# Dense layers on float16 halves with scales taken from the data, and every weight chunk used once for all 1792 tokens

## The chip, the cores and the metric

The kernel runs on one core of a Trainium2 chip. The metric is the device time of one execution in microseconds (us); before the change it is 1415.47 us, the median of 3 runs between 1414.61 and 1416.2. The engines are TensorE (PE in the profile, its weight loads PEld), VectorE (DVE), ScalarE (ACT), GpSimd (POOL) and SyncE (SP), which here only issues DMAs.

## The reference

Talking-heads attention, then two dense blocks on its result (1792 tokens = 4 batches x 448, width 768 = 12 heads x 64):

```python
scores = einsum('bhij,hg->bgij', q @ k.T * 0.125, w_pre)
attn = softmax(scores)
x = einsum('bhij,hg->bgij', attn, w_post) @ v     # -> [1792, 768]
h = (x @ w1) * (x @ w2)                           # w1, w2: 768 x 1024
x2 = h @ w3 @ w_out                               # 1024 x 1024, 1024 x 768
g = relu(x2 @ w_in) ** 2                          # 768 x 2048
out = g @ moe2_w_out                              # 2048 x 768, float32
```

The attention inputs are float32. The dense weights arrive as float64, and the kernel reads them as pairs of int32.

## The kernel before

The first part, up to about 493 us, is the attention: 180 blocks (16 supers of 11 or 12 blocks, four to a batch) in an order written out by hand, slot by slot, with later steps attached to slots by `at()`. Of it only its output step matters here: `put_x` (L452) scales the finished rows on ACT and sends them to DRAM as float32 (`xT_d`), `regroup` (L259) is a DMA that each block needs four slots ahead, and `load_x` (L688) brings x back for the dense part.

The dense part is scheduled by the Tile framework, engine by engine, from the order of the code. Its products take float32 in two fp32r parts, a high one (`wh`, `hh`) and the rest (`wl`, `ll`), and add three matmuls: high x high, high x low, low x high (`product`, L784, 448 columns; `layer_out`, L904, and `m_pair`, L809, 384 columns). A weight chunk is decoded from float64 by two ACT activations, an integer step, a clamp, a second integer step on DVE, an Abs on ACT and a product with the sign on DVE (L622 to L632); then ACT rounds the high part (L661) and POOL subtracts (L662).

The tokens go through in two halves of 896 (the loop `for hf in range(NH)`). Half 0 decodes each chunk and keeps the decoded float32 in DRAM (`kept_*`, L654); half 1 loads these again and splits them on ACT and DVE (L648, L649). Once, between the w1/w2 products and x2 of half 0, M = w3 @ w_out is formed from 384 matmuls and put into DRAM (`M_d`); x2 = h @ M. In the last part p runs over 8 pairs of chunks: `layer_in(2p)`, `layer_in(2p+1)` and then `layer_out(p-1)`, whose products DVE adds into the accumulator (L912; at p = 0 ACT copies, L910). PSUM gives the dense part 8 banks (`mm`).

Of the kernel before, what the change touches and what calls it, by code (L numbers as in the profile page):

```python
# [1 line left out]

# [26 lines left out]
WO_AT = (1, 2, 4, 5)  # L29


@with_exitstack
def talking_heads_attention_moe_moe2(
# [39 lines left out]
    xT_d = dram.tile([DM, NT], F32, name="xT_d")  # L73
    M_d = dram.tile([NDC, P, NFC * P], F32, name="M_d")
# [7 lines left out]
    const = ctx.enter_context(tc.tile_pool(name="const", bufs=1))  # L82
    sp = ctx.enter_context(tc.tile_pool(name="sp", bufs=2))
# [303 lines left out]
    def scale_v(b, hg, i):  # L387
        m = vsum[b, hg]
        if i == 0:
            nc.vector.tensor_reduce(m[:CP, 3:4], m[:CP, 0:3], axis=AX.X, op=ALU.max)  # L390
        elif i == 1:
            vps[b, hg] = pt = psum(ps_p, "p")
            nc.tensor.transpose(pt[:1, :CP], m[:CP, 3:4], ident[:CP, :CP])
        elif i == 2:
            pt = vps.pop((b, hg))
            nc.vector.tensor_reduce(m[:1, 4:5], pt[:1, :CP], axis=AX.X, op=ALU.max)
        elif i == 3:
            vps[b, hg] = pt = psum(ps_p, "p")
# [99 lines left out]
    for b in range(B):  # L498
        f = first[4 * b]
        for hg, o in ((0, 2), (1, 8)):  # L500
            at(f + o - 5, LOAD, load_v, b, hg)
            for i in range(3):
                at(f + o + i + 1, MID, sum_v, b, hg, i)
                at(f + o + i + 9, MID, split_v, b, hg, i)
                at(f + o + i + 10, LOW, split_vl, b, hg, i)
            for i, (slot, kind) in enumerate(((4, MID), (5, END), (6, MID), (7, END), (8, MID))):
                at(f + o + slot, kind, scale_v, b, hg, i)
    for s in range(NSUP - 1):
        L = -(-SUP[s + 1][2] // NR)
# [39 lines left out]
    for hf in range(NH):  # L549
        for fc in range(NFC):  # L550
            chunks += [("w1", hf, fc), ("w2", hf, fc)]
            if hf == 0 and fc in WO_AT:
                j = 2 * WO_AT.index(fc)
                chunks += [("wo", 0, j), ("wo", 0, j + 1)]
        if hf == 0:
            for p in range(NFC // 2):
                for g in range(2):
                    chunks += [("w3", 0, 4 * p + 2 * j + g) for j in range(2)]
                if p == 0:
                    chunks += [("wo", 1, f) for f in range(NFC // 2, NFC)]  # L560
        for c in range(NDC):
            chunks += [("m", hf, 2 * c), ("m", hf, 2 * c + 1)]
        for p in range(NP2):
            chunks += [("in", hf, 2 * p), ("in", hf, 2 * p + 1)]
            if p > 0:
                chunks += [("out", hf, 2 * p - 2), ("out", hf, 2 * p - 1)]
        chunks += [("out", hf, NF2 - 2), ("out", hf, NF2 - 1)]
# [8 lines left out]
    limit = [place["wo", 1, NFC // 2]]

    def in_place(i):
        return chunks[i][0] == "m" or chunks[i][1] > 0

    def wtile(z):
        return pools["w"].tile([P, DM], F32R, tag=f"w{z}", name=f"w{z}", bufs=WBUFS)

    def load_w(i):
        kind, hf, j = chunks[i]
        cs = slice(j * P, (j + 1) * P)
        if in_place(i):
            if kind == "wo":
                t = wo_tiles(j)[1]
            else:  # L590
                t = wtile("l")
            if kind == "m":
                c, g = divmod(j, 2)
                lo, hi = (0, MF * P) if g == 0 else (MF * P, (NFC if hf else NFC - 2) * P)
                t = t[:, : hi - lo]
                nc.sync.dma_start(t.bitcast(F32), M_d[c][:, lo:hi])
            else:
                nc.sync.dma_start(t.bitcast(F32), kept[kind, j])
            wraw[i] = t
            return  # L600
        t = pools["w"].tile([P, 2 * DM], I32, tag="raw", name="raw", bufs=LOADS)
        if kind in ("out", "wo"):
            src = {"out": moe2_w_out, "wo": moe_w_out}[kind].bitcast(I32)
            nc.sync.dma_start(t, src[cs, :])
        elif kind == "w3":
            f, g = divmod(j, 2)
            t = t[:, : 8 * P]
            nc.sync.dma_start(t, moe_w3.bitcast(I32)[f, g])
        else:
            src = {"w1": moe_w1, "w2": moe_w2, "in": moe2_w_in}[kind].bitcast(I32)  # L610
            nc.sync.dma_start(t, src[j])
        wraw[i] = t

    def decode(raw, n):
# [381 lines left out]
```

## Time and profile before

| | |
|---|---|
| median of 3 runs | 1415.47 us (1414.61 to 1416.2) |
| the profiled execution's own time | 1411.23 us |
| its span, first to last instruction | 1409.5 us |
| mean granted TensorE clock | 0.985 |
| PE busy | 1358.5 us, 96% of the span, 10176 matmuls |
| DVE / ACT / POOL busy | 983.7 (70%) / 745.2 (53%) / 497.9 us (35%) |
| HBM read / written | 100.49 MB / 34.60 MB |

A share of busy time is a mean over stages: attention, then w1/w2, M, x2 and in/out. A matmul's duration in the timeline is a latency; matmuls overlap, and what each costs is the distance between two starts. In the tables of windows the columns are busy us and number of instructions of each engine, then the granted clock (1.00 is the 2.4 GHz level, 0.50 the 1.2 GHz level), the share of time in which the DMA engines work, and GB/s.

### The profile page before, as it was taken

What the parts mean: (1) busy time and instruction counts of PE and PEld (TensorE: products, weight loads), DVE (VectorE), ACT (ScalarE), POOL (GpSimd) and SP (SyncE); (2) the same over time, 40 slices, a digit from 0 to 9 for tenths busy, and PEclk for the clock granted to TensorE, in tenths of its full rate; (3) what the DMA queues carried; (4) which work ended last, traced back from release to release, by engine and by line L of the source; (5) the groups of instructions that cost most, each with busy time, mean ns of one, the idle gap of its engine ahead of it and who ended that gap; (6) DMA issues with size and microseconds to landing.
All of it is one profiled execution on the core that took longest, in us unless ns stands there. A gap on an engine that the chain in (4) does not pass through costs nothing. (4 is left out here: it accounts for less than half of the span.)

```text
span 1409.5 us, 26306 instructions
## 1 busy us (share of the span) xinstructions
PE 1358.5 (96%) x10176; PEld 1155.9 (82%) x10176; DVE 983.7 (70%) x1688; ACT 745.2 (53%) x1363; POOL 497.9 (35%) x489
## 2 busy tenths in 40 slices
PE   5999999999998799889999999999999999999999
PEld 3566666666665599789999999999999999999998
DVE  6998999999898877865627788998322224355555
ACT  3877877877875766665526655554222223422220
POOL 3789789789775623222102222221000000000000
PEclk8999999999999799999999999999999999999999
DMA  5345445455537456644524344434211121111112
GB/s 174 109 136 151 117 136 154 127 138 145 143 89 226 147 188 204 221 160 135 189 73 169 129 174 169 157 124 162 96 57 53 38 66 57 57 45 47 66 57 90
DMA packets 82512, 175.32 MB, mean 124 GB/s; under 512 B 19412, under 2 KB 51540, under 8 KB 82388
## 3 DMA queue, kind: packets, MB, share of 16 engines
q1 hardware_dynamic: 82388, 173.65, 39.5%
q8 instruction: 80, 1.31, 0.4%
q14 instruction: 44, 0.36, 0.1%
HBM read 100.49 MB, written 34.60 MB: 96 GB/s over the span
## 5 line engine op out<-in xcount | busy, mean ns | idle before, releaser
L784 PE MATMUL mm<-hl,wh 128*128 128x448 f32 x1536 | 443.8, 370 | 2.6 <-ACT wh L661 1.5
L784 PEld LDWEIGHTS mm<-hl,wh 128*128 128x128 f32 x1536 | 290.1, 189 | 31.0 <-ACT wh L661 2.2
L784 PE MATMUL mm<-hl,wl 128*128 128x448 f32 x768 | 284.4, 370 | 2.9 <-POOL wl L662 2.9
L904 PE MATMUL mm<-wh,act 128*128 128x384 f32 x896 | 231.8, 337 | 0.9 <-ACT act L910 0.6
L339 PEld LDWEIGHTS <-EH 120*112 120x112 f16 (+1 forms) x1440 | 134.5, 132 | 86.9 <-issue 86.6
L265 PE MATMUL p<-Bt,wpre_k 120*120 120x448 f32 x360 | 183.6, 593 | 15.7 <-DMA Bt<-S 13.0
L327 POOL TENSOR_TENSOR EL<-E,EH 120x448 f16<-120x448 f32 x180 | 191.4, 1064 | 15.0
L662 POOL TENSOR_TENSOR wl<-xa,wh 128x768 fp32r<-128x768 f32 x48 | 89.9, 1880 | 288.3 <-ACT wh L661 261.6
L904 PEld LDWEIGHTS mm<-wh,act 128*128 128x128 f32 x896 | 162.2, 188 | 2.8 <-DVE act L912 1.3
L324 POOL TENSOR_SCALAR E<-E,st 120x448 f32<-120x448 f32 x180 | 135.4, 752 | 75.1 <-DVE EH L316 33.8
L784 PEld LDWEIGHTS mm<-hl,wl 128*128 128x128 f32 x768 | 145.3, 189 | 17.8 <-POOL wl L662 3.7
L904 PE MATMUL mm<-wl,act 128*128 128x384 f32 x448 | 150.6, 336 | 0.0
L287 ACT ACTIVATE E<-p,st 120x448 f32<-120x448 f32 x180 | 115.3, 640 | 58.6 <-DVE st L279 46.4
L648 ACT CAST wh<-wl 128x768 fp32r<-128x768 f32 (+1 forms) x72 | 53.5, 746 | 156.0 <-DMA wl<-kept_out 73.2
L339 PE MATMUL o<-wph,EH 120*112 120x120 f16 x720 | 127.2, 219 | 7.3 <-DVE ATl L361 6.8
L339 PE MATMUL o<-wph,EL 120*112 120x120 f16 x720 | 127.0, 219 | 3.1 <-POOL EL L327 2.8
L912 DVE TENSOR_TENSOR act<-act,mm 128x384 f32<-128x384 f32 x196 | 103.1, 550 | 37.9 <-PE mm L904 37.2
L279 DVE TENSOR_REDUCE st<-p 120x1 f32<-120x448 f32 x180 | 110.9, 616 | 25.7 <-PE p L265 23.9
L339 PE MATMUL o<-wpl,EH 120*112 120x120 f16 x720 | 127.1, 219 | 0.0
L649 DVE TENSOR_TENSOR wl<-wl,wh 128x768 fp32r<-128x768 f32 (+1 forms) x72 | 60.4, 845 | 90.7 <-ACT wh L648 88.2
L355 ACT CAST ATh<-o 112x480 f16<-112x480 f32 x180 | 100.9, 560 | 43.0 <-PE o L339 42.1
L316 DVE TENSOR_SCALAR EH<-E,st 120x448 f16<-120x448 f32 x180 | 121.2, 673 | 2.9
(128 smaller groups left out, 2490.7 us busy)
## 6 DMA issues: line engine op xcount, KB each, us to landing
Bt<-S SPq DMA_DIRECT2D x176, 210.0 KB
raw<-in_moe_w_out_dram SPq DMA_DIRECT2D x24, 768.0 KB
raw<-in_moe_w_dram SPq DMA_DIRECT2D x16, 768.0 KB
raw<-in_moe_w_in_dram SPq DMA_DIRECT2D x16, 768.0 KB
raw<-in_moe_w_dram SPq DMA_DIRECT2D x16, 512.0 KB
kept_w<-xa SPq DMA_DIRECT2D x16, 384.0 KB
kept_in<-xa SPq DMA_DIRECT2D x16, 384.0 KB
kept_out<-xa SPq DMA_DIRECT2D x16, 384.0 KB
```

The lines of the kernel that those rows point to most:

```text
L265: nc.tensor.matmul(pt[: n * H, :S], wpre_k.rearrange("p t g -> p (t g)")[: n * H, : n * H], Bt.pop(u)[: n * H], start=True, stop=True,)
L279: nc.vector.tensor_reduce(nsum[u][:n, 0, j : j + 1], Pp[u][:n, :S], axis=AX.X, op=ALU.max, negate=True)
L287: nc.scalar.activation(e[:n], Pp.pop(u)[:n, :S].rearrange("p (a b) -> p a b", a=EG), AF.Exp, bias=t[:n, 0, j : j + 1], scale=1.0, accum_ou ...
L316: nc.vector.tensor_scalar(hh[:n].rearrange("p (a b) -> p a b", a=EG), Ex[u][:n], inverse(u), None, op0=ALU.mult)
L324: nc.gpsimd.tensor_scalar(e, e, inverse(u), 1.0, op0=ALU.mult, op1=ALU.mult)
L327: nc.gpsimd.tensor_tensor(a, e, b, op=ALU.subtract)
L339: nc.tensor.matmul(pt[:CP, c * n : (c + 1) * n], a[:n, c * CP : (c + 1) * CP], w[:n, :n], start=(i == 0), stop=(i == 2),)
L355: nc.scalar.copy(ATs[s][0][:, :, :, m * NR : m * NR + nr], src)
L662: nc.gpsimd.tensor_tensor(ll, x, hh, op=ALU.subtract)
L784: nc.tensor.matmul(pt[:, :S], w[a][:, cs], x[z][:, sl], start=(c == 0 and i == 0), stop=(c == len(parts) - 1 and i == 2),)
L904: nc.tensor.matmul(pt[:, :OH], gs[j][a][:, ts_], ws[j][w][:, os_], start=(n == 0), stop=(n == 5),)
L912: nc.vector.tensor_tensor(acc[t][:, os_], acc[t][:, os_], pt[:, :OH], op=ALU.add)
```

## The change

The dense products go to float16 parts, high and low again, three matmuls each. So that they fit the range of float16, each operand is multiplied by a power of two found from the data: a maximum over the free axis by DVE (`largest`), a maximum over the 128 partitions by a round trip through DRAM (`across`: a write of [128, n], a read of all of it into every partition, a reduce on DVE), and four small DVE instructions (`pow2`). These scales are needed for each pair of weight chunks, for M, for each batch of x2 and for each pair of g. The M stage itself stays in fp32r. The loop over halves, the `kept_*` copies except four, and `M_d` go away: each weight chunk is decoded and used once for 1792 tokens. The attention writes x as two float16 parts (`put_xh` on ACT, `put_xl` on DVE), and computes the scale of v once a batch instead of twice; the last two of its 16 supers write x straight into SBUF.

```diff
-        nc.scalar.activation(xt[:, :, :R], src, AF.Copy, scale=un)
-        nc.sync.dma_start(
-            xT_d[3 * hg * P : (3 * hg + 3) * P, b * S + r0 : b * S + r0 + R].rearrange(
-                "(j p) r -> p j r", p=P
-            ),
-            xt[:, :, :R],
-        )
+    def put_xh(s, hg):
+        if s >= NSUP - 2:
+            xt = [z[:, 3 * hg : 3 * hg + 3, b * S + r0 : b * S + r0 + R] for z in xall]
...
+        nc.scalar.activation(xt[0], src, AF.Copy, scale=2.0 ** -XSH)
+    def put_xl(s, hg):
+        nc.vector.scalar_tensor_tensor(
+            xt[1], src, 2.0 ** -XSH, xt[0], op0=ALU.mult, op1=ALU.subtract
+        )
+        if s < NSUP - 2:
+            for z in range(2):
+                nc.sync.dma_start(x_d[z, b, :, 3 * hg : 3 * hg + 3, r0 : r0 + R], xt[z])
+    def load_x():
+        for b in range(B):
+            n = S if b < B - 1 else sum(ROWS[:-2])
+            for z in range(2):
+                nc.sync.dma_start(xall[z][:, :, b * S : b * S + n], x_d[z, b, :, :, :n])
...
+    def across(src, n, dma, together=False):
+        d = dram.tile([P, n], F32, name=f"across_{ncross[0]}")
+        dma.dma_start(d, src)
+        t = sm.tile([P, P * 4], F32, tag="ac", name="ac")[:, : P * n]
+        dma.dma_start(
+            t, d.rearrange("p n -> (p n)").unsqueeze(0).to_broadcast([P, P * n])
+        )
+        m = 1 if together else n
+        r = sm.tile([P, 4], F32, tag="acr", name="acr")[:, :m]
+        nc.vector.tensor_reduce(
+            r, t.rearrange("p (q n) -> p n q", n=m), axis=AX.X, op=ALU.max
+        )
+        return r
...
+    def pair_steps(i, dma=None):
+        def begin(k):
+            x, ops = decode(wraw.pop(i + k), DM, tot[:, k : k + 1])
...
+        def scale():
+            r = across(tot, 2, dma or nc.gpsimd, kind == "out")
+            res.append(pow2(r, 14, "ws", n) + (n,))
+        def cast(k, z):
+            if z == 0:
+                nc.scalar.activation(w[:, 0], xx[k], AF.Copy, scale=up[:, c : c + 1])
+            else:
+                nc.vector.scalar_tensor_tensor(
+                    w[:, 1], xx[k], up[:, c : c + 1], w[:, 0], op0=ALU.mult, op1=ALU.subtract
+                )
...
+        if u == NB - LEAD + 1:
+            load_x()
...
+    def halves(t, x, up):
+        h, l = t
+        nc.scalar.activation(h, x, AF.Copy, scale=up)
+        nc.vector.scalar_tensor_tensor(l, x, up, h, op0=ALU.mult, op1=ALU.subtract)
+    def largest(out, x):
+        nc.vector.tensor_reduce(out, x, axis=AX.X, op=ALU.max, apply_absolute_value=True)
...
-    for hf in range(NH):
...
+    mup, mlo = pow2(across(mx[:, :1], 1, nc.sync), 14, "ms")
+    for o in range(2):
+        for f in range(NFC):
+            os_ = slice(o * OH, (o + 1) * OH)
+            halves([z[:, os_] for z in M16[f]], M32[f][o][:, :OH], rows[:, 3, f : f + 1])
...
+    def layer_in(f, gm, j):
+            nc.scalar.activation(t, pt[:, :S], AF.Relu, scale=sc[:, i : i + 1])
+            nc.vector.tensor_tensor(g, t, t, op=ALU.mult)
+            largest(gm[:, i, j : j + 1], g)
...
+                if p == 0:
+                    nc.scalar.activation(d, pt[:, :OH], AF.Copy, scale=sv[:, v : v + 1])
                 else:
-                    parts.append((w[f // MF], cols_of(f % MF), hs[f]))
+                    nc.vector.scalar_tensor_tensor(
+                        d, pt[:, :OH], sv[:, v : v + 1], d, op0=ALU.mult, op1=ALU.add
+                    )
...
+    for p in range(NP2):
+        raws = [layer_in(2 * p + j, gm, j) for j in range(2)]
+        nc.vector.tensor_reduce(gx, gm, axis=AX.X, op=ALU.max)
+        up, lo = pow2(across(gx, B, nc.gpsimd), 14, "gs", B)
+        for j in range(2):
+            t = fin.tile([P, 2, NT], F16, tag="g", name="g", bufs=4)
+            for i in range(B):
+                halves((t[:, 0, toks(i)], t[:, 1, toks(i)]), raws[j][i], up[:, i : i + 1])
+            gs.append(two(t))
+        if p + 1 < NP2:
+            need(("in", 2 * p + 3))
+        need(("out", 2 * p + 1))
+        if prev is not None:
+            layer_out(p - 1, *prev)
+        prev = (gs, lo)
```

The names of the rows below are the program's; line numbers of the changed kernel are its own. First, SP's queue in the last slots of the attention, before: the loads of x (L692, `hl<-xT_d`) stand between the DMAs that the blocks need (L259).

```order
L259 DMA Bt_8158<-S_7624 120x1x448 [waits DMAHW3_49,Activation_49]
L692 DMA hl_9249<-xT_d_57 128x896 [waits DMAHW6_49,DMAHW7_49,DMAHW4_49,DMAHW0_49]
L259 DMA Bt_8197<-S_7624 120x1x448 [waits PE_49]
L692 DMA hl_9249<-xT_d_57 128x896
L259 DMA Bt_8239<-S_7624 120x1x448 [waits DMAHW5_49,PE_49]
L692 DMA hl_9249<-xT_d_57 128x896 x3
```

And the same queue in the changed kernel.

```order
L262 DMA Bt_8492<-S_7566 120x1x448 [waits DMAHW2_49,PE_49]
L262 DMA Bt_8548<-S_7566 120x1x448 [waits DMAHW3_49,PE_49]
L262 DMA Bt_8589<-S_7566 96x1x448 [waits DMAHW5_49,DMAHW4_49,PE_49]
L491 DMA x_8648<-x_d_57 128x6x448
L491 DMA x_8649<-x_d_57 128x6x448 [waits DMAHW3_49,DMAHW4_49,DMAHW2_49,DMAHW6_49,DMAHW1_49,DMAHW0_49]
L491 DMA x_8648<-x_d_57 128x6x448 [waits DMAHW7_49]
L491 DMA x_8649<-x_d_57 128x6x448
L491 DMA x_8648<-x_d_57 128x6x448
L491 DMA x_8649<-x_d_57 128x6x448
L491 DMA x_8648<-x_d_57 128x6x220
L491 DMA x_8649<-x_d_57 128x6x220
L642 DMA across_1_8864<-tot_8473 128x2 [waits DMAHW5_49,Activation_49]
```

The loads now stand in one piece behind the last of the blocks' DMAs, with the round trip of the first weights behind them. Then ACT of the changed kernel at the same place; `x_8648` is the high part of x, `E` and `ATh` are steps of the attention's last blocks.

```order
L290 ACTIVATE E_8596,st_8594<-p_8551,st_8594 120x7x64 [waits DVE_49,Activation_49,Pool_49]
L623 ACTIVATE zt_8621<-raw_8328 128x768 [waits DMAHW4_49]
L358 CAST ATh_8446<-o_8605 112x48x10 [waits PE_49]
L470 ACTIVATE x_8648<-a_8479 128x3x110 [waits DMAHW3_49,DMAHW2_49,DMAHW7_49,DMAHW0_49,PE_49]
L290 ACTIVATE E_8663,st_8594<-p_8592,st_8594 120x7x64 [waits DVE_49,Pool_49]
L624 ACTIVATE zs_8622<-raw_8328 128x768 [waits Activation_49]
L358 CAST ATh_8446<-o_8670 112x48x10 [waits PE_49]
```

Before, ACT's row of this step (L457) waited for PE and for the DMA out of its own buffer; now it waits for the loads into the tile that it writes to, with five of the attention's steps of the last two blocks behind it. Next, DVE in one `layer_out` before (L912 is the eviction of a PSUM tile, the rest decodes the next chunks).

```order
L912 TENSOR_TENSOR act_11811<-act_11811,mm_12669 128x384 [waits PE_49]
L628 SCALAR_TENSOR_TENSOR xa_12836<-zt_12834,xa_12836 128x768 [waits DVE_49]
L912 TENSOR_TENSOR act_11811<-act_11811,mm_12677 128x384 [waits PE_49]
L912 TENSOR_TENSOR act_11828<-act_11828,mm_12685 128x384 [waits PE_49]
L632 TENSOR_TENSOR xa_12836<-xa_12836,zs_12835 128x768 [waits Activation_49]
L912 TENSOR_TENSOR act_11828<-act_11828,mm_12693 128x384 [waits PE_49]
L912 TENSOR_TENSOR act_11845<-act_11845,mm_12701 128x384 [waits PE_49]
```

And DVE in the `layer_out` of p = 2 in the changed kernel, from the seventh eviction (L1018) on: L649 is the reduce behind a round trip, L863 are the low halves of g, L681 the low parts of two weight chunks.

```order
L1018 SCALAR_TENSOR_TENSOR acc_13446<-mm_14010,sv_13956,acc_13446 128x384 [waits PE_49]
L649 TENSOR_REDUCE acr_13847<-ac_13845 128x4 [waits DMASW6_49]
L649 TENSOR_REDUCE acr_13897<-ac_13895 128x2 [waits DMASW7_49]
...
L1018 SCALAR_TENSOR_TENSOR acc_13479<-mm_14042,sv_13956,acc_13479 128x384 [waits PE_49]
L863 SCALAR_TENSOR_TENSOR g_13854<-st_13667,gs_13849,g_13854 128x448 [waits Activation_49]
...
L863 SCALAR_TENSOR_TENSOR g_13863<-st_13837,gs_13849,g_13863 128x448 [waits Activation_49]
L681 SCALAR_TENSOR_TENSOR w_13904<-xa_13873,ws_13899,w_13904 128x768 [waits Activation_49]
L681 SCALAR_TENSOR_TENSOR w_13907<-xa_13883,ws_13899,w_13907 128x768 [waits Activation_49]
L625 TENSOR_SCALAR xa_13915<-raw_13910 128x768 [waits DMAHW3_49,DVE_49]
L625 TENSOR_SCALAR xa_13925<-raw_13912 128x768 [waits DMAHW4_49,DVE_49]
L629 SCALAR_TENSOR_TENSOR xa_13915<-zt_13916,xa_13915 128x768 [waits DVE_49]
L1018 SCALAR_TENSOR_TENSOR acc_13479<-mm_14050,sv_13956,acc_13479 128x384 [waits PE_49]
```

Before, at most two steps of a decode stood between two evictions; now the twelfth eviction stands behind two waits for a DMA, eight halves, two casts and three steps of a decode. Last, ACT before, where it casts the weights of p = 0 (L661) among the evictions of `layer_in` (L886).

```order
L661 CAST wh_11702<-xa_11693 128x768 [waits PE_49]
L886 ACTIVATE ta_11616<-mm_11597 128x448 [waits PE_49,Activation_49]
L888 CAST act_11570<-th_11617 128x448 [waits DVE_49]
L631 ACTIVATE xa_11779<-xa_11779 128x768 [waits DMAHW3_49,DVE_49,Pool_49]
L886 ACTIVATE ta_11660<-mm_11641 128x448 [waits PE_49]
```

And ACT of the changed kernel between `layer_in(1)` (L983 is its eviction) and `layer_in(2)`, whose weight is `w_13043`; `gs` is the scale of g.

```order
L983 ACTIVATE st_12975<-mm_12956,sci_12882 128x448 [waits DVE_49,PE_49]
L862 ACTIVATE g_12993<-st_12806,gs_12988 128x448 [waits DVE_49]
L862 ACTIVATE g_12993<-st_12830,gs_12988 128x448
...
L862 ACTIVATE g_13002<-st_12976,gs_12988 128x448
L678 ACTIVATE w_13043<-xa_13012,ws_13038 128x768 [waits DVE_49]
L678 ACTIVATE w_13046<-xa_13022,ws_13038 128x768
```

The weight that PE needs next is now cast behind the eight halves of g, and these behind the round trip of g's maximum.

## Rows read from the trace of the kernel before

**Rows 1.** Table of windows: end of attention, start and long stretch of the dense part.

```profile
400.00:430.00 30.00, 30.00 (x376) 20.53 (x375) 29.55 (x57) 23.50 (x50) 23.28 (x27) 1.00 0.37 101
430.00:440.00 10.00, 9.29 (x135) 6.70 (x135) 9.86 (x19) 6.17 (x16) 7.44 (x10) 1.00 0.89 271
440.00:492.00 52.00, 37.24 (x654) 29.48 (x652) 43.24 (x75) 34.00 (x63) 31.18 (x29) 0.81 0.57 171
490.00:495.00 5.00, 3.88 (x57) 3.51 (x52) 2.30 (x4) 5.00 (x8) 3.36 (x2) 0.50 0.92 338
1000.00:1400.00 400.00, 400.00 (x2041) 373.95 (x2040) 163.32 (x256) 107.17 (x177) 0.00 (x0) 1.00 0.17 55
```

**Rows 2.** Instructions of the tile mm: count, min/median/max ns, first and last start.

```profile
L784 PE MATMUL mm<-hl,wh x1536: 362/369/742, 492.8 to 1376.2; 128*128 128x448 f32 x192
```

**Rows 3.** Table of windows for line 784 alone, columns PE, PEld, clock, DMA.

```profile
492.00:1409.50 917.50, 600.49 (x2880) 543.41 (x2880) 0.99 0.34 115
```

**Rows 4.** The same for line 904.

```profile
492.00:1409.50 917.50, 236.67 (x1344) 233.16 (x1344) 0.99 0.34 115
```

**Rows 5.** Timeline of PE, matmuls of 448 columns: start, duration, engine, line, operands, count.

```profile
999.84 0.57 PE L784 MATMUL mm<-hl,wh 128*128 128x448 f32 x2
...
1003.56 0.57 PE L784 MATMUL mm<-hl,wh 128*128 128x448 f32 x2
```

**Rows 6.** Timeline of PE, matmuls of 384 columns.

```profile
1390.00 0.51 PE L904 MATMUL mm<-wh,act 128*128 128x384 f32 x2
...
1395.72 0.51 PE L904 MATMUL mm<-wh,act 128*128 128x384 f32 x2
```

**Rows 7.** Timeline of PE in the attention, float16 matmuls of 120 columns.

```profile
300.36 0.22 PE L339 MATMUL o<-wph,EH 120*112 120x120 f16 x1
...
300.94 0.22 PE L339 MATMUL o<-wph,EL 120*112 120x120 f16 x1
```

**Rows 8.** Timeline, last eviction of the kernel.

```profile
1405.98 0.55 DVE L912 TENSOR_TENSOR act<-act,mm 128x384 f32<-128x384 f32 x1 [0.49 <-PE mm L904]
```

**Rows 9.** Timeline of DVE, blocks 171 and 177 of 180 (their max).

```profile
440.26 0.61 DVE L279 TENSOR_REDUCE st<-p 120x1 f32<-120x448 f32 x1
...
461.68 0.61 DVE L279 TENSOR_REDUCE st<-p 120x1 f32<-120x448 f32 x1
```

**Rows 10.** Timeline, the first load of q and the instruction that waits for it.

```profile
0.81 0.38 SPq L190 DMA_DIRECT2D qraw<-in_q_dram  x1
...
3.79 0.57 DVE L201 CAST qh<-qraw 128x330 fp32r<-128x330 f32 x2 [3.79 <-DMA qraw<-in_q_dram]
```

**Rows 11.** Timeline of DVE, steps of a decode and of a layer's eviction.

```profile
862.08 2.18 DVE L624 TENSOR_SCALAR xa<-raw 128x768 int32<-128x768 int32 x1 [0.26 <-POOL wl L662]
...
866.63 0.95 DVE L632 TENSOR_TENSOR xa<-xa,zs 128x768 f32<-128x768 f32 x1
867.50 0.62 DVE L887 TENSOR_TENSOR th<-ta 128x448 f32<-128x448 f32 x1
868.04 0.55 DVE L627 TENSOR_SCALAR zt<-zt 128x768 f32<-128x768 f32 x1
868.51 0.95 DVE L632 TENSOR_TENSOR xa<-xa,zs 128x768 f32<-128x768 f32 x1
...
887.78 2.41 DVE L912 TENSOR_TENSOR act<-act,mm 128x384 f32<-128x384 f32 x5
```

**Rows 12.** Timeline of DVE, a small instruction on two values a partition.

```profile
309.70 0.17 DVE L308 RECIPROCAL st<-st 120x2 f32<-120x2 f32 x1
```

**Rows 13.** Timeline of ACT, a cast of 448 columns and the next of 768.

```profile
546.05 0.57 ACT L854 CAST act<-th 128x448 fp32r<-128x448 f32 x1
546.51 0.85 ACT L661 CAST wh<-xa 128x768 fp32r<-128x768 f32 x1
```

**Rows 14.** POOL: a long subtraction of the attention, and the mean of all (groups: busy, mean ns).

```profile
473.31 3.49 POOL L327 TENSOR_TENSOR EL<-E,EH 120x448 f16<-120x448 f32 x1
...
L327 POOL TENSOR_TENSOR EL<-E,EH 120x448 f16<-120x448 f32 x180 | 191.4, 1064 | 15.0
```

More of the change, by code (lines that the diff above doesn't have):

```diff
@@ L537, in talking_heads_attention_moe_moe2 @@
             evict_s(0, p)
-    NH = 2
-    TH = NT // NH
-    NB2 = TH // S
     NP2 = NF2 // 2
-    MF = 4
     pools = {}
     chunks = []
-    for hf in range(NH):
[L550 to L567, printed above, removed]
+    for fc in range(NFC):
+        chunks += [("w1", fc), ("w2", fc)]
+        if fc in WO_AT:
+            j = 2 * WO_AT.index(fc)
+            chunks += [("wo", j), ("wo", j + 1)]
@@ L573, in talking_heads_attention_moe_moe2 @@
     wraw, wsp = {}, {}
-    LOADS, SPLITS, WBUFS = 3, 2, 4
+    LOADS = 2
     done = [0, 0]
[L576 to L582, printed above, removed]
-    def load_w(i):
[L585 to L589, printed above, removed]
-            else:
[L591 to L611, printed above, removed]
@@ L637, in split_w, with split_one @@
+    WB = 7
+    def split_one(i):
+        kind, j = chunks[i]
         t = wraw.pop(i)
         if kind == "w3":
-            x = decode(t, 4 * P)
-            dh, dl = wtile("h")[:, : 4 * P], wtile("l")[:, : 4 * P]
+            x, ops = decode(t, 4 * P)
+            for f in ops:
+                f()
+            dh, dl = (
+                pools["w"].tile([P, 4 * P], F32R, tag="w", name="w3", bufs=WB) for _ in range(2)
+            )
             nc.scalar.copy(dh, x)
@@ L752, in talking_heads_attention_moe_moe2 @@
         if p % 3 == 2:
-            put_x(last, p // 3)
+            put_xh(last, p // 3)
+            put_xl(last, p // 3)
+    for f in early:
+        f()
     order.close()
-    need(chunks[0], 0)
-    need(chunks[1], 0)
-    xs_next = load_x(0)
     bst.close()
@@ L796, in toks, with two @@
         return slice(i * S, (i + 1) * S)
-    M_last = {}
-    def m_pair(p):
+    def two(t):
+        return t[:, 0], t[:, 1]
+    def halves(t, x, up):
[4 more added lines that the diff above has]
+        nc.vector.tensor_reduce(out, x, axis=AX.X, op=ALU.max, apply_absolute_value=True)
+    x16 = [(xall[0][:, c], xall[1][:, c]) for c in range(NDC)]
+    rows = sm.tile([P, 4, NFC], F32, tag="rows", name="rows", bufs=1)
@@ new lines, in talking_heads_attention_moe_moe2 @@
+    kx = sm.tile([P, B], F32, tag="kx", name="kx", bufs=1)
+    hs = []
+    for fc in range(NFC):
+        ws = [need((kind, fc)) for kind in ("w1", "w2")]
+        sc = sm.tile([P, 2, B], F32, tag="sc", name="sc")
+        for z in range(2):
+            nc.vector.tensor_scalar(sc[:, z], xs, ws[z][1], None, op0=ALU.mult)
+        hm = sm.tile([P, B + 1], F32, tag="hm", name="hm")
+        ths = []
+        for i in range(B):
+            pt = [mm(), mm()]
+            for z in range(2):
+                product(pt[z], [(two(ws[z][0]), cols_of(c), x16[c]) for c in range(NDC)], toks(i))
+            ta, th = stage(), stage()
+            nc.scalar.activation(ta, pt[0][:, :S], AF.Copy, scale=sc[:, 0, i : i + 1])
+            nc.vector.scalar_tensor_tensor(
+                th, pt[1][:, :S], sc[:, 1, i : i + 1], ta, op0=ALU.mult, op1=ALU.mult
+            )
+            largest(hm[:, i : i + 1], th)
+            ths.append(th)
+            if i == 0:
+                need(chunks[min(place["w2", fc] + (4 if fc in WO_AT else 2), place["w2", NFC - 1])])
+        nc.vector.tensor_reduce(hm[:, B : B + 1], hm[:, :B], axis=AX.X, op=ALU.max)
+        up, lo = pow2(hm[:, B : B + 1], 14, "hs")
+        nc.vector.tensor_copy(rows[:, 0, fc : fc + 1], lo)
+        t = mlp.tile([P, 2, NT], F16, tag="h", name="h", bufs=NFC)
+        for i in range(B):
+            halves((t[:, 0, toks(i)], t[:, 1, toks(i)]), ths[i], up)
+        hs.append(two(t))
@@ new lines, in talking_heads_attention_moe_moe2 @@
+    mx = sm.tile([P, 2], F32, tag="mx", name="mx")
+    nc.vector.tensor_reduce(mx[:, :1], rows[:, 2], axis=AX.X, op=ALU.max)
+    mup, mlo = pow2(across(mx[:, :1], 1, nc.sync), 14, "ms")
+    nc.vector.tensor_scalar(rows[:, 3], rows[:, 0], mup, None, op0=ALU.mult)
+    M16 = []
+    for f in range(NFC):
+        M16.append(two(mp.tile([P, 2, DM], F16, tag="m", name="M16")))
+    for o in range(2):
+        for f in range(NFC):
+            os_ = slice(o * OH, (o + 1) * OH)
+            halves([z[:, os_] for z in M16[f]], M32[f][o][:, :OH], rows[:, 3, f : f + 1])
@@ new lines, in talking_heads_attention_moe_moe2 @@
+    xb = [sp.tile([P, NDC, NT], F16, tag="S", name="x2") for _ in range(2)]
+    x2 = [(xb[0][:, c], xb[1][:, c]) for c in range(NDC)]
+    for i in range(B):
+        xm = sm.tile([P, NDC + 1], F32, tag="xm", name="xm")
+        ts = []
+        for c in range(NDC):
+            pt = mm()
+            product(pt, [(M16[f], cols_of(c), hs[f]) for f in range(NFC)], toks(i))
+            t = stage()
+            nc.scalar.activation(t, pt[:, :S], AF.Copy, scale=mlo)
+            largest(xm[:, c : c + 1], t)
+            ts.append(t)
+        nc.vector.tensor_reduce(xm[:, NDC:], xm[:, :NDC], axis=AX.X, op=ALU.max)
+        up, lo = pow2(across(xm[:, NDC:], 1, nc.sync), 14, "xs")
+        nc.vector.tensor_copy(kx[:, i : i + 1], lo)
+        for c in range(NDC):
+            halves([z[:, toks(i)] for z in x2[c]], ts[c], up)
+        if i == 0:
+            need(("in", 1))
```

436 lines of the change are left out of this document (224 added, 212 removed).

## Prediction

> **What bounds the kernel now.** I read the table of windows first [rows 1]. From 1000 to 1400 us PE is busy the whole 400 us at clock 1.00, DVE 163, ACT 107, POOL nothing: the dense part is bound by the number of matmuls times the distance between them. Just before 430 us PE is full too, but DVE with 29.55 of 30 us is no less so; from 430 the loads of x, of weights and of the blocks' own operands share DMA at 0.89 of its time and 271 GB/s, and between 440 and 492 PE works only 37.24 of 52 us. Next the row of the tile mm: the dense part starts at 492.8 [rows 2]. It has 2880 matmuls of 448 columns [rows 3] and 1344 of 384 [rows 4], besides 384 of 384 columns that form M. The timelines of PE give the distances: 18 matmuls from 999.84 to 1003.56, 206.7 ns each at 448 columns [rows 5], 33 from 1390.00 to 1395.72, 173.3 ns each at 384 [rows 6]. So the matmuls need 2880 x 0.2067 + (1344 + 384) x 0.1733 = 894.8 us of the 913.2 between 492.8 and the last eviction at 1406.0 [rows 8]; 18 us are stalls and slow clock.
>
> **The product itself.** The number of dense matmuls stays: 1152 (w1, w2) + 576 (x2) + 1152 (w_in) = 2880, and 8 x 14 x 2 x 6 = 1344. What changes is their type. The only float16 row is the attention's: 11 distances in 0.58 us, 52.7 ns for 120 columns [rows 7]. At 2.4 GHz 120 columns are 50.0 ns, so 2.7 ns are added, against 20 at 448 fp32r columns (186.7) and 13.3 at 384 (160). I take 186.7 + 2.7 = 189.4 and 162.7 ns. The other bound is fp32r's own distance (no gain). Gain: 2880 x 0.0173 + 1344 x 0.0106 = 49.8 + 14.2 = 64 us. M's 384 matmuls keep 0.1733: 66.6 us.
>
> Halving the weight traffic (no reload, no second split on ACT and DVE, no POOL subtraction L662 for most chunks) costs and gives nothing by itself, since PE hides it today [rows 1]. What it buys is spent on scales: DVE has now per step p two `layer_in` (8 tiles x (0.54 + 0.61)), 8 low halves of 0.54, 28 evictions of 0.48, four chunks of two steps of 0.47 and three of 0.87, and smalls of 0.2, in all some 46 us (0.54, 0.47, 0.87 from distances of starts, 0.48 from five in 2.41 [rows 11]; 0.61 [rows 9]; 0.2 [rows 12]) against 27.3 + 27.3 = 54.6 us of PE. On average DVE isn't the bound; its order is.
>
> **The transition.** All x except the last supers, 4.8 MB, is loaded in one piece, behind the last of the blocks' DMAs. At 271 GB/s that is 18 us. ACT's `x_8648` (L470), DVE's low part and with them the softmax steps of the last two blocks wait for it. Against that, the stretch 440 to 492, where 14.8 us of PE are lost today to just such loads, runs free until then: blocks 171 to 177 take 21.4 us today [rows 9]; six blocks at 2.35 (430 us over 180 blocks, rounded down) are 14.1, 7.3 less. So the loads start near 454 and land near 474, at about block 178.5; from block 177 to the dense start are 31.1 us today, of which some 23 are left there, without the split of x (now done) but with the first round trip in DVE's queue ahead of the last block's `EH`. I take 498, range 488 (the wait is covered) to 505. The attention's own new work on DVE (`put_xl`, 16 x 0.5) less the saved scales of v is some 3 us, hidden but for DVE's full stretch.
>
> **The round trip.** No row shows a DMA issued by POOL, nor a round trip. One leg: 2.98 us from q's first load to the instruction that waits for it, 338 KB [rows 10]; last eviction ended (1406.5) to the end of the span (1409.5), 3.0 us. Two legs are 6.0; without the bytes (338 KB at 271 GB/s, 1.25) a leg is 1.75, two are 3.5. The write is tiny, the read of 128 x 512 values is 262 KB: 4.5 to 6.0, I take L = 5.5 for POOL's, 4.3 for SP's with fewer bytes. Upwards: POOL and DVE disturb each other. One subtraction of POOL took 3.49 us against 1.06 on average [rows 14], and one DVE step of usually 0.55 took 2.18, behind a POOL step [rows 11]. Two legs delayed by 2.4 each make L = 10.8.
>
> The Trainium skill speaks against the change here: SBUF — State Buffer, section "SBUF: two separate sides", says that a DMA issued from POOL can't have its descriptors written while DVE is in a mode that takes both ports, the lock being exclusive for an instruction. Rows 14 bear out that such blocking exists between instructions; whether descriptors suffer no row shows. By the fixed 2.0 us and 436 GB/s that DMA: Bandwidth & Descriptors gives in "Anatomy of one DMA — SWDGE (gpsimd) path", the trip would be an estimated 4.6 us, and the sum some 7 us lower.
>
> **Where PE meets it.** w1/w2: the scale of a pair is asked for a pair ahead, 8 banks are 27 us of matmuls; only the cold start, 3 us (granted clock 0.50 in 490 to 495 [rows 1]). M to x2: PE's last matmul to the first half of M needs copies and maxima (2.6), SP's trip (4.3), smalls (1.0), one ACT half and its hand-over (0.8): 8.7, and 2 for the clock after the pause, 10.7. x2 to in: the last batch's scale has three batches of cover, 0.5. Steps p = 0 to 1: `w_13043` stands on ACT behind eight halves and the trip: eviction, square, max (2.0), L, the two reduces (1.0), smalls (1.4), 8 x 0.46 and a cast of 0.85 [rows 13] = L + 9.0 = 14.5, and 2 for the clock: 16.5. p = 1: ACT evicts, 0.5. From p = 2 to 6 DVE's twelfth eviction stands behind trip, halves and casts. Counted from the last matmul of `layer_in`: 2.0 + L + four evictions and smalls 4.4 + halves 4.3 + casts 1.75 + decode 1.8 + eviction 0.5 + hand-overs between ACT and DVE 2.1 = 22.4. PE runs on through eight banks and wants the twelfth's again at 19 x 0.976 = 18.5. Stall 3.9, with the clock 4.4; five times, 22. p = 7: 2. Together 41, and 8 us for each us of L.
>
> **Sum.** Start 498; w1/w2 1152 x 0.1894 + 3 = 221.2; M 66.6 + 2.5 = 69.1; to x2 10.7; x2 576 x 0.1894 + 0.5 = 109.6; in and out 1152 x 0.1894 + 1344 x 0.1627 = 436.9; stalls 41; last eviction and store 3.0 [rows 8]. Span 1389.5, own time with the 1.7 us around it 1391, against 1411.2. The runs' median lies 4.2 above the profiled execution: **1396 us**.
>
> **Rivals.** (B) The trip is short, L = 4 or less, or the scheduler's order lets more evictions pass than I count; the start comes at 490 to 493. For it: PE has 18 us of banks, a shortage of 3.9 is within the error of my 22.4. Against it: 4.5 is two legs with bytes. Stalls 28 or less, start 6 earlier: about 1376. (C, slower) A trip started from POOL takes 10 us or more, as DVE is at work 46 of 54.6 us and holds what POOL needs: the place is DVE's waiting reduce (L649) with the evictions behind it, in each `layer_out` from p = 2, and the pause at p = 0. 41 + 4.8 x 8.7 = 83: about 1438. It is what the lock of the Trainium skill's page above would come to here. It decides from L = 8 on: the 20 us of forecast gain are 2.5 us of L. For it: rows 14; against: POOL has almost no other work in the dense part now, and only whole instructions of under 1 us are in its way. (D) The float16 matmul of 448 columns isn't closer spaced than the fp32r one: 64 us are lost, about 1460. For it: 2.7 is taken from 120 columns on a 112-row result; against: if the distance had a floor or a further term, 52.7 ns leave no place for it.
>
> **Chances.** Forecast 0.45, B 0.28, C 0.22, D 0.05. This kernel's measurement tells about 0.2% from no change, 1412.6 to 1418.3. The forecast's own range, L from 4.5 to 7.5 and the start 488 to 505, is 1380 to 1412; to hold 8 in 10 it takes in B and half of C: 1366 to 1440. Faster: B, nearly all of the forecast: 0.68. Same: the strip between forecast and C, 0.07. Slower: C and D less that strip, 0.25.
>
> **What would show it.** In the profile after: distances of 189 and 163 ns in the float16 products (207 would be D); one gap of PE of some 15 us after `layer_in(1)`, ended by ACT's cast of w (L678); one of some 9 ahead of x2; five of some 4 in `layer_out`, ended by DVE's evictions (L1018), with the reduce L649 waiting for a DMA ahead of them; ACT's L470 idle some 15 us for the loads of x, and the first dense matmul near 498. Gaps of 10 in each `layer_out` are C; none, B. Wrong would be the forecast also if PE waited in w1/w2, where I count on 27 us of cover.

## The result and the profile after

The changed kernel takes 1434.3 us (median of 4 runs, 1428.17 to 1435.94) against 1415.43: ratio of the runs 1.0126, 95% interval 1.0095 to 1.0156. It is slower, by a little over 1%; the forecast was 1396, faster. The profiled execution has a span of 1432.7 us against the 1389.5 of the sum, 43 more (38 between the medians).

The gain that was forecast is there. Timeline of PE in the changed kernel, which groups equal matmuls into one row:

```profile
879.77 4.51 PE L842 MATMUL mm<-h,M 128*128 128x448 f16 x23
...
1004.80 7.48 PE L1009 MATMUL mm<-w,g 128*128 128x384 f16 x45
```

Less the latency of the last one (352 and 326 ns by the groups) that is (4.51 - 0.35)/22 = 189 ns and (7.48 - 0.33)/44 = 162.6 ns, against 206.7 and 173.3 [rows 5, 6]: 64 us over all matmuls. The dense part starts at 498.5, as the sum had it (492.8 before [rows 2]):

```profile
L842 PE MATMUL mm<-x,w x2304: 349/352/581, 498.5 to 1370.2; 128*128 128x448 f16 x192
```

Yet the dense part takes 934.2 us, against 916.7 before: the 64 us are given back, and 17 more, by pauses of PE and the slow clock behind them. These are rows of the same timeline that carry an idle time (in brackets, with what ended it), one of each kind:

```profile
664.25 3.56 PE L842 MATMUL mm<-x,w 128*128 128x448 f16 x18 [1.72 <-ACT st L885]
...
810.20 4.29 PE L842 MATMUL mm<-h,M 128*128 128x448 f16 x11 [16.12 <-ACT M L862]
936.97 0.53 PE L842 MATMUL mm<-x,w 128*128 128x448 f16 x1 [5.02 <-ACT x L862]
972.68 0.93 PE L842 MATMUL mm<-x,w 128*128 128x448 f16 x2 [16.18 <-ACT w L678]
1022.82 1.62 PE L1009 MATMUL mm<-w,g 128*128 128x384 f16 x6 [3.88 <-ACT acc L1016]
1086.04 4.32 PE L1009 MATMUL mm<-w,g 128*128 128x384 f16 x13 [3.92 <-DVE acc L1018]
...
1391.01 5.25 PE L1009 MATMUL mm<-w,g 128*128 128x384 f16 x21 [1.96 <-DVE acc L1018]
```

In the w1/w2 part there are six of the kind of the first, 0.55 to 1.72 and 5.9 us together; of the 3.92 there are five, one in each `layer_out` from p = 2 to 6, 3.82 to 3.92. Behind each long pause the clock is at the lower level for some us. Table of windows, same columns as in rows 1:

```profile
440.00:492.00 52.00, 35.97 (x561) 28.71 (x563) 39.89 (x79) 24.60 (x53) 27.65 (x28) 0.73 0.74 196
...
1000.00:1400.00 400.00, 374.80 (x2049) 206.11 (x2048) 300.56 (x599) 162.79 (x260) 21.87 (x40) 0.95 0.18 55
...
974.00:976.00 2.00, 2.00 (x7) 0.78 (x6) 2.00 (x4) 0.00 (x0) 0.00 (x0) 0.50 0.00 0
...
1086.04:1091.60 5.56, 5.56 (x18) 2.69 (x18) 5.55 (x9) 4.09 (x8) 0.55 (x1) 0.50 0.63 225
```

The stretch 1000 to 1400, all PE at 1.00 before [rows 1], has lost 25 us of PE and runs at 0.95; DVE has risen from 163 to 301. In 974 to 976 PE passes for fully busy, but has 7 matmuls in it, where 2 us at clock 1.00 have 12 (window 982 to 984 of the run on the clock, below). Behind the pause of 3.92 the lower level lasts 5.56 us, half of which, 2.8, is lost.

The trips themselves, ahead of x2 (issued by SP) and after `layer_in(1)` (by POOL): write, read, and the reduce that waits for it.

```profile
796.45 0.33 SPq L642 DMA_DIRECT2D across<-mx  x1
803.57 0.33 SPq L644 DMA_DIRECT2D ac<-across  x1
808.18 0.29 DVE L649 TENSOR_REDUCE acr<-ac 128x1 f32<-128x128 f32 x1 [11.76 <-DMA ac<-across]
...
958.98 0.55 POOL L642 DMA_DIRECT2D across<-gx  x1 [90.44 <-DVE gx L1029]
960.97 1.14 POOL L644 DMA_DIRECT2D ac<-across  x2 [1.45 <-DMA across<-gx]
965.11 1.37 DVE L649 TENSOR_REDUCE acr<-ac 128x4 f32<-128x512 f32 x2 [6.43 <-DMA ac<-across]
```

POOL's trip takes 6.1 us, close to the L = 5.5 taken. SP's takes 11.7, where 4.3 was taken, with a quarter of the bytes; 7.1 of it is the write (over SP's five trips of this kind, 6.6 to 8.2 from the write's issue to that of the read, which waits for it). The table of DMA issues (KB each, median us to landing) says what goes with it:

```profile
across<-tot POOLq DMA_DIRECT2D x23, 1.0 KB, 3.6
...
across<-gx POOLq DMA_DIRECT2D x8, 2.0 KB, 1.7
```

4 bytes a partition 6.6 to 8.2 us (SP), 8 bytes 3.6, 16 bytes 1.7 (POOL): the fewer bytes, the longer.

### The profile page after: what moved, and what is told of

The parts are those of the page before. It is cut to its first block, busy times and chain, and to the rows that moved or that the text cites. A ratio compares the mean times of both kernels' runs of the same rounds, so it can differ in the third digit from the quotient of the medians.

```text
span 1432.7 us, 26336 instructions
## 1 busy us (share of the span) xinstructions
PE 1310.3 (91%) x10164; PEld 796.6 (56%) x10164; DVE 1056.4 (74%) x2138; ACT 728.9 (51%) x1365; POOL 442.2 (31%) x503
## 5 line engine op out<-in xcount | busy, mean ns | idle before, releaser
L842 PE MATMUL mm<-x,w 128*128 128x448 f16 x2304 | 447.3, 357 | 29.1 <-ACT w L678 16.2
L842 PEld LDWEIGHTS <-w 128*128 128x128 f16 x2304 | 227.2, 99 | 247.4 <-issue 24.9
L1009 PE MATMUL mm<-w,g 128*128 128x384 f16 x1344 | 238.1, 342 | 25.2 <-DVE acc L1018 21.3
L1009 PEld LDWEIGHTS <-g 128*128 128x128 f16 x1344 | 137.3, 102 | 125.3 <-issue 45.3
L1018 DVE SCALAR_TENSOR_TENSOR acc<-mm,sv,acc 128x384 f32<-128x384 f32 x196 | 115.2, 610 | 20.2 <-PE mm L1009 19.9
L842 PE MATMUL mm<-h,M 128*128 128x448 f16 x576 | 111.5, 358 | 16.1 <-ACT M L862 16.1
L364 DVE TENSOR_TENSOR ATl<-o,ATh 112x480 f16<-112x480 f32 x180 | 116.2, 646 | 2.4 <-ACT ATh L358 2.1
L649 DVE TENSOR_REDUCE acr<-ac 128x2 f32<-128x256 f32 (+3 forms) x37 | 19.2, 539 | 132.9 <-DMA ac<-across 132.9
L632 ACT ACTIVATE xa<-xa 128x768 f32<-128x768 f32 (+1 forms) x72 | 57.3, 796 | 100.3 <-DVE xa L629 60.4
L239 ACT COPY S<-s 110x896 f32<-110x896 f32 (+1 forms) x92 | 83.7, 910 | 24.6 <-PE s L228 21.8
```

Source lines behind the costliest of these rows:

```text
L364: nc.vector.tensor_tensor(ATs[s][1][:, :, :, a], src, ATs[s][0][:, :, :, a], op=ALU.subtract)
L842: nc.tensor.matmul(pt[:, :S], w[a][:, cs], x[z][:, sl], start=(c == 0 and i == 0), stop=(c == len(parts) - 1 and i == 2),)
L1009: nc.tensor.matmul(pt[:, :OH], gs[j][a][:, ts_], ws[j][0][:, w, os_], start=(n == 0), stop=(n == 5),)
L1018: nc.vector.scalar_tensor_tensor(d, pt[:, :OH], sv[:, v : v + 1], d, op0=ALU.mult, op1=ALU.add)
```

## The experiments

The theory: the trips and the queue orders around them make the pauses, and each long pause costs the slow clock behind it besides. Rivals, by run: DVE's order or its time makes them, SP is the slow issuer, the slow start behind a pause is something else than the clock. The ratios stand against runs of the kernel before on the same chip, 1414.0 us for e1 to e4 and 1414.4 for e5 to e8.

**No trip (e1).**

```diff
-        dma.dma_start(d, src)
...
-        nc.vector.tensor_reduce(
-            r, t.rearrange("p (q n) -> p n q", n=m), axis=AX.X, op=ALU.max
-        )
+        nc.vector.tensor_copy(r, src[:, :m])
```

> across() keeps each partition's own maximum (copy on DVE) in place of the round trip through DRAM; the maximum over the 128 partitions is left out, all other instructions stay. Theory (the trips and the slow clock behind each pause cost the gain): the pause ahead of x2 falls from 16.1 to 4 to 5 us, that in layer_in of the first chunk (5.0) and those of the w1/w2 part (5.9 in all) go, the one after layer_in(1) falls from 16.2 to about 9, the five of 3.9 in layer_out go with the 2.2 us of half clock behind each: 1434 - 12 - 7 - 8 - 30 - 6 and some us at the start = about 1365 us. Rival (DVE's order alone, with the halves and casts ahead of the twelfth eviction, makes the pauses): they stay at 3 us or more, total 1410 or more.

1370.4 us, ratio 0.9691 (0.9662 to 0.9720): 64 us less than the changed kernel. The pauses that remain:

```profile
783.30 4.88 PE L833 MATMUL mm<-h,M 128*128 128x448 f16 x16 [4.27 <-ACT M L853]
930.06 0.93 PE L833 MATMUL mm<-x,w 128*128 128x448 f16 x2 [8.70 <-ACT w L669]
1029.05 5.25 PE L1000 MATMUL mm<-w,g 128*128 128x384 f16 x21 [2.08 <-DVE acc L1009]
```

16.1 fell to 4.3 and 16.2 to 8.7 as expected, 5.0 and those of w1/w2 are gone. In `layer_out` the theory failed in part: 2.1 stay and not none, since halves and casts stand in one piece ahead of an eviction even without a trip (now ahead of the sixth: the scheduler's order moved with the edit). With the slow clock or small pauses behind it each still costs 3.5 to 4.0 us, of 6.6. So order has a share of its own.

**Bytes a partition, or the issuer (e2, e3).** Two runs. The first repeats the values to four columns before each trip; the second moves the trips of M and x2 to POOL.

```diff
+        if n < 4:
+            s4 = sm.tile([P, 4], F32, tag="s4", name="s4", bufs=4)
+            for k in range(0, 4, n):
+                nc.vector.tensor_copy(s4[:, k : k + n], src)
+            src = s4
+        d = dram.tile([P, 4], F32, name=f"across_{ncross[0]}")
...
```

> every round trip writes 16 bytes a partition (the values repeated to four columns) in place of 4 or 8, and reads 256 KB. Theory (the write is slow because many partitions write few bytes into the same stretch of DRAM: 7 to 8 us at 4 bytes, 3.6 at 8, 1.7 at 16): SP's writes land in about 2 us, the pause ahead of x2 falls from 16.1 to about 11, the one of 5.0 goes; weights' trips 1 to 2 us shorter; total 1412 to 1422. Rival (a DMA of SP is the slow one): writes of x2 and M stay at 7 to 8 us, total 1432 to 1438.

```diff
-    mup, mlo = pow2(across(mx[:, :1], 1, nc.sync), 14, "ms")
+    mup, mlo = pow2(across(mx[:, :1], 1, nc.gpsimd), 14, "ms")
...
-        up, lo = pow2(across(xm[:, NDC:], 1, nc.sync), 14, "xs")
+        up, lo = pow2(across(xm[:, NDC:], 1, nc.gpsimd), 14, "xs")
```

> the round trips of M and x2 (4 bytes a partition) are issued by POOL in place of SP, nothing else. Theory (bytes a partition): the write still takes about 7 us, pauses stay near 16 and 5, total 1430 to 1440. Rival (SP's path is slow, POOL's fast): write about 2 us, trips about 6, total 1420 to 1425.

Wide: 1407.4 us, 0.9953 (0.9935 to 0.9972), 27 us less, more than the 12 to 22 expected. Issued by POOL: 1436.8, 1.0172 (1.0137 to 1.0208), no gain. Of the wide run, the weights' writes, the pause ahead of x2 and the two in the `layer_out` of p = 2; of the other, the writes of x2 and the pause ahead of it:

```profile
across<-s POOLq DMA_DIRECT2D x23, 2.0 KB, 1.7
...
802.75 3.58 PE L847 MATMUL mm<-h,M 128*128 128x448 f16 x10 [10.56 <-ACT M L867]
...
1066.64 2.11 PE L1014 MATMUL mm<-w,g 128*128 128x384 f16 x12 [1.05 <-DVE acc L1023]
1071.40 4.77 PE L1014 MATMUL mm<-w,g 128*128 128x384 f16 x18 [2.66 <-DVE acc L1023]
```

```profile
across<-xm POOLq DMA_DIRECT2D x4, 0.5 KB, 7.5
...
811.75 4.66 PE L842 MATMUL mm<-h,M 128*128 128x448 f16 x12 [17.68 <-ACT M L862]
```

The issuer is cleared: 4 bytes take 7.5 us from POOL too, 16 bytes 1.7 from POOL and 1.5 to 2.8 from SP. With the wide writes the pause ahead of x2 fell to 10.6, and the one of 5.0 and those in w1/w2 went. The pause after `layer_in(1)` stayed at 16.5, since g's trip was wide already. The gain beyond the forecast lies in `layer_out`, where the scheduler's order moved with the edit: two evictions now stand between the halves and the casts, and pauses and slow clock of p = 2 to 6 come to some 24 us in place of 33.

**Is it the small piece, or that neighbours share a stretch of DRAM? (e5)**

```diff
+        if n == 1:
+            d = dram.tile([P, 16], F32, name=f"across_{ncross[0]}")
+            dma.dma_start(d[:, :1], src)
...
+            dma.dma_start(t, d[:, 0].unsqueeze(0).to_broadcast([P, P]))
```

> the round trips of M and x2 still write 4 bytes a partition from SP, but each partition at its own 64 bytes of DRAM, and read them back at that pitch. Theory (the write is slow because neighbours share a stretch of DRAM): the read is issued about 2 us after the write, in place of 7 to 8. Rival (it is the size of each piece alone, wherever it goes): still 7 to 8 us. The total is no test, since the read now gathers 128 x 128 single values and may be slower.

1440.65 us (one run). Timeline, the trip ahead of x2:

```profile
804.24 0.33 SPq L643 DMA_DIRECT2D across<-mx  x1
805.71 0.38 SPq L645 DMA_DIRECT2D ac<-across  x1
817.04 0.29 DVE L647 TENSOR_REDUCE acr<-ac 128x1 f32<-128x128 f32 x1 [12.83 <-DMA ac<-across]
```

The read is issued 1.5 us after the write, not 7.1 (the four trips of x2: 1.5, 3.7, 2.2, 1.5, against 6.6 to 8.2): the same 4 bytes are fast once they lie apart. What was won goes into the gathering read, 11.3 us where the plain one took 4.6.

**Order (e4).**

```diff
-        up, lo = pow2(across(gx, B, nc.gpsimd), 14, "gs", B)
+        end = across_start(gx, B, nc.gpsimd)
...
+            layer_out(p - 1, *prev)
+        up, lo = pow2(end(), 14, "gs", B)
         gs = []
```

> the reduce at the end of g's round trip and the eight halves of g come after layer_out(p-1) in the code, so that the order puts the evictions first; the trip is started where it was. Theory (a queue order, cured without touching a trip): the five pauses of 3.9 us and their slow clock go (30 us), the pause after layer_in(1) falls to about 12: total about 1400. Rival (DVE hasn't the time: the halves and casts then delay layer_in or the next layer_out as much): 1425 or more, with new pauses ended by DVE g.

1400.25 us, 0.9898 (0.9871 to 0.9926), as the theory had it. The five pauses are gone; those ahead of x2 and of 5.0 stay (16.8 and 6.0), and in the part with in and out the largest left are

```profile
971.92 2.35 PE L849 MATMUL mm<-x,w 128*128 128x448 f16 x5 [11.84 <-ACT w L685]
...
1021.58 0.65 PE L1016 MATMUL mm<-w,g 128*128 128x384 f16 x3 [3.44 <-ACT acc L1023]
```

DVE had the time: no new pause is ended by its halves. The first row's 11.8 is the 12 of the forecast.

**Weights of the second pair earlier (e8).**

```diff
+        if i == 2:
+            need(("in", 3))
```

> the changed kernel with chunks 2 and 3 of w_in asked for during x2 (one need() more), nothing else. Theory (the pause after layer_in(1) is ACT's cast of w behind the halves of g): the 16.2 us and 3.4 us of half clock go: about 1415. Rival (the pause is g's own round trip, and moves to the next wait for g, at layer_out(0)): 1428 or more.

1422.7 us, 1.0065 (1.0043 to 1.0087), between the two. The pause after `layer_in(1)` is gone, but two others have grown, from 5.0 and 3.9:

```profile
944.23 0.53 PE L842 MATMUL mm<-x,w 128*128 128x448 f16 x1 [9.31 <-ACT x L862]
1012.73 5.60 PE L1011 MATMUL mm<-w,g 128*128 128x384 f16 x17 [5.39 <-ACT acc L1018]
```

So 16.2 was ACT's cast in its queue, as the rows of the order said, and 5.8 us of it were given back at other trips.

**The clock (e7).**

```diff
+    busy_pe(80)
     xb = [sp.tile([P, NDC, NT], F16, tag="S", name="x2") for _ in range(2)]
...
+        if p == 0:
+            busy_x(80)
```

> the changed kernel with 80 extra float16 matmuls (15.2 us) whose result nobody reads, in the pause ahead of x2 and again in the one after layer_in(1); nothing else. Theory (PE's half clock behind a pause is a cost of its own, 2.4 and 3.4 us): both pauses keep their length, the matmuls behind them are 189 ns apart from the first on, total about 1428. Rival (what is slow behind the pause is the supply of halves, not the clock): no gain or a loss, 1433 to 1438.

1438.7 us, 1.0172 (1.0153 to 1.0191): the forecast of the total failed. The local part held. Windows of this kernel behind the two filled pauses:

```profile
819.00:821.00 2.00, 1.57 (x8) 0.58 (x8) 1.70 (x4) 2.00 (x5) 0.00 (x0) 1.00 0.32 66
...
982.00:984.00 2.00, 2.00 (x12) 1.00 (x11) 2.00 (x4) 0.00 (x0) 0.00 (x0) 1.00 0.00 0
```

At clock 1.00 from the start, x2 takes 109.1 us from its first matmul to its last (111.2 in the changed kernel), and from the second pair's first `layer_in` matmul to the first of `layer_out(0)` it is 28.0 us (30.5). So 2.1 and 2.5 us were the clock's and not the supply's. But the pause ahead of x2 was 1.1 us longer, the dense part began 5.3 us later in this profile, and the pause in `layer_out(0)` was 6.6 in place of 3.9. The start differs by several us between these kernels (492.2 to 504.4), also where nothing ahead of it was edited. Most of that stands already inside the attention, which no run edits: the maximum of block 151 of 180, of the changed kernel and of this one:

```profile
394.85 0.62 DVE L282 TENSOR_REDUCE st<-p 120x1 f32<-120x448 f32 x1
```

```profile
398.86 0.62 DVE L282 TENSOR_REDUCE st<-p 120x1 f32<-120x448 f32 x1
```

So 4 of the 5.3 us have nothing to do with the extra matmuls, and a total alone can't show an effect of 2 to 5 us here; where those 4 us come from is open.

**All cures together (e6)**, 16-byte writes, late halves, early weights:

> 16-byte writes in every trip, the halves of g behind layer_out, and the weights of chunks 2 and 3 of w_in asked for during x2, before layer_in(0). Theory (named pauses and the half clock behind them): from 1400 of the late halves, 6 less ahead of x2, 8 less in the first layer_in, 6 less in w1/w2, 15 less after layer_in(1), 2 or 3 more at the start: about 1367. Rival (DVE's time is then the bound): 1385 or more with new pauses.

1359.5 us, 0.9613 (0.9598 to 0.9627): 55 us faster than the kernel before, 75 than the changed one. The cures alone gave 27, 34 and 12, together 73. That the whole is so near their sum is partly chance: some 9 us of the wide writes' gain lie in the pauses that the late halves remove as well, while the early weights keep here what they alone gave back at other trips. One pause of over 2 us is left in the dense part, and the long stretch of in and out is PE's:

```profile
801.39 0.93 PE L854 MATMUL mm<-h,M 128*128 128x448 f16 x2 [10.82 <-ACT M L874]
...
912.00:1350.00 438.00, 436.04 (x2482) 242.55 (x2480) 357.49 (x736) 179.59 (x293) 23.97 (x44) 1.00 0.22 68
```

DVE is busy 357 of 438 us there without stopping PE. The rival that its time is the bound is out.

## Why the prediction was wrong

By its steps:

- **The product**, 64 us from closer matmuls: right to under a nanosecond each. Rival D is out.
- **The transition**, start at 498: measured 498.5, by luck. The stretch from 440 to 492 didn't run free of loads: PE is busy 35.97 us there, 37.24 before [rows 1], and blocks 171 to 177 take 19.0 us (their maxima at 441.86 and 460.85), where 14.1 were taken. ACT's L470, which the order shows waiting for the loads, found them done. The loads of x held SP's queue from 455.1 to 470.4, near the forecast; the first trip behind them went out at 472.9, when ACT's last step of the first decode (L632) let it. DVE waited for it, with the last block's `EH` behind it, and ACT for a weight chunk queued behind the trip's write.

```profile
455.08 15.37 SPq L491 DMA_DIRECT2D x<-x_d  x8
472.90 0.34 SPq L642 DMA_DIRECT2D across<-tot  x1
...
482.02 0.89 ACT L623 ACTIVATE zt<-raw 128x768 f32<-128x768 f32 x1 [8.70 <-DMA raw<-in_moe_w_dram]
...
482.39 0.42 DVE L649 TENSOR_REDUCE acr<-ac 128x2 f32<-128x256 f32 x1 [6.24 <-DMA ac<-across]
```

  So what held the start was this trip, 9.5 us from write to reduce, which the prediction names but doesn't price. Without it (e1) the dense part starts at 492.2, though block 151 stands at the same 394.9.

- **In and out from p = 2**: stall 3.9 forecast, 3.82 to 3.92 measured, at the twelfth eviction, and e4 shows the mechanism. That it fits to a tenth is partly luck. These are rows of ACT, POOL and DVE at p = 2: last eviction of `layer_in`, trip, reduce, halves, twelfth eviction.

```profile
1063.64 0.63 ACT L983 ACTIVATE st<-mm,sci 128x448 f32<-128x448 f32 x1 [2.77 <-PE mm L842]
1066.87 0.55 POOL L642 DMA_DIRECT2D across<-gx  x1 [17.23 <-DVE gx L1029]
1072.81 1.40 DVE L649 TENSOR_REDUCE acr<-ac 128x4 f32<-128x512 f32 x2 [1.72 <-DMA ac<-across]
1076.94 4.86 DVE L863 SCALAR_TENSOR_TENSOR g<-st,gs,g 128x448 f16<-128x448 f32 x8
1085.38 1.13 DVE L1018 SCALAR_TENSOR_TENSOR acc<-mm,sv,acc 128x384 f32<-128x384 f32 x2
```

  To the trip it is 3.2 us, where 2.0 were taken, the trip is 5.9; and the 2.1 for hand-overs between ACT and DVE isn't there, as the eight halves follow without a gap. The errors cancel. By the same sum no stall would be left without a trip, yet e1 has 2.1. p = 0 to 1: 14.5 forecast, 16.2 measured.
- **The trip of POOL**, L = 5.5: 6.1. Rival C, POOL held up by DVE, came near in time (1438) but by chance: its sign, gaps of 10 in each `layer_out`, isn't there, and with DVE busier than before POOL's write of g lands in 1.7 us. So no starving of descriptors of the kind that the Trainium skill describes (SBUF — State Buffer, section "SBUF: two separate sides") is to be seen here; as DVE mostly evicts from PSUM or waits during these trips, the runs say little of the lock itself.
- **The failed step is "Where PE meets it"**, in four of its terms. First, SP's trip: 4.3 taken, 11.7 measured, +7.4 ahead of x2; I had put its price below POOL's for its fewer bytes, and the fewer bytes made it dearer (e2, e3, e5). Second, x2 to in: "three batches of cover, 0.5"; the cover was 10.4 us of matmuls, and the last batch's trip of 11.8 us outlasted it: a pause of 5.0 and 2.1 of slow clock, +6.6. Third, the clock: 0.5 us behind a pause of 3.9, 2 behind a long one; measured 2.7 to 2.8 behind the five of `layer_out` and 2.1 to 3.2 behind the long ones (e7 gave 2.1 and 2.5 back at two of these). Over the five that is +11. Fourth, cover counted in banks alone: in w1/w2 ("only the cold start") and at p = 1 ("ACT evicts, 0.5") ACT's evictions stand behind casts or halves that wait for a trip, the very thing that I had priced on DVE: +6 and +5. ACT in w1/w2 and at p = 1, where L885 and L1016 are the evictions:

```profile
662.74 0.93 ACT L678 ACTIVATE w<-xa,ws 128x768 f16<-128x768 f32 x1 [7.23 <-DVE ws L113]
663.58 0.62 ACT L885 ACTIVATE st<-mm,sc 128x448 f32<-128x448 f32 x1
...
1016.07 4.58 ACT L862 ACTIVATE g<-st,gs 128x448 f16<-128x448 f32 x8 [4.31 <-DVE gs L113]
1020.56 1.75 ACT L678 ACTIVATE w<-xa,ws 128x768 f16<-128x768 f32 x2
1022.21 1.96 ACT L1016 ACTIVATE acc<-mm,sv 128x384 f32<-128x384 f32 x4
```

These make some 36 of the 43 us; another 3 are p = 0 to 1, and the rest lies in p = 7, the end and slow clock in w1/w2, less 2.2 of the 2.5 that the sum gives to M without a row (M took 66.9). No term alone turned the sign: the forecast gain was 20 us, and the two largest of these sums with any third undo it.

## What to carry to other kernels

A gain in matmul distance is worth what the queues leave of it: where a scale needs a maximum over partitions, start the trip early, and put everything that waits for it behind the evictions in the code, on every engine that evicts, not only on the busiest. A pause of PE of some 4 us cost 5.5 to 6.7 here, with the clock behind it. The scheduler's order moves with an edit: read it again in each run. Don't write 128 values of 4 bytes side by side to DRAM in a latency chain: write 16 bytes a partition and read them back whole.

## What the runs showed of the hardware

The landing time of a small DMA into DRAM rises as the piece of each partition shrinks: 1.7 us at 16 bytes, 3.6 at 8 (POOL; 5.0 in the one from SP), 6.6 to 8.2 at 4, from SP or POOL alike, and 1.5 to 3.7 at 4 bytes with 64 from one to the next. Size alone isn't it; pieces that lie close together seem to wait for one another. The Trainium skill (DMA: Bandwidth & Descriptors, Specifications) has it that a transfer under 512 bytes is read, modified and written. That fits pieces that share a stretch, but the pieces at a pitch of 64 are under 512 bytes too and land fast, and at what grain sharing hurts these runs don't tell. A read that gathers 4 bytes at a pitch of 64 took 11.3 us against 4.6 for the packed one.
